# w_out*phi tiles converted around the border of chunks 0 and 1, and g of chunk 1 in the buffer of chunk 0's x

## The chip, the cores and the metric

The kernel runs on one core of a Trainium2 chip. The metric is the device time of one execution in microseconds; the time of the kernel before is the median of three runs.

## The reference

Three stages follow each other on 2304 tokens (4 batches of 576) of 512 features: an attention with 8 heads (four local, four strided), a feed-forward layer, and a soft mixture of 8 experts with 4 slots each.

```python
x = attention(q, k, v)                        # masked, 8 heads, (2304, 512)
h = x @ w_in                                  # (2304, 2048)
g = h * (1.0 / (1.0 + np.exp(-1.702 * h)))
x = g @ w_out                                 # (2304, 512)
logits = x @ phi                              # 32 slots
d = softmax(logits, over tokens); slot_input = d.T @ x
for e in range(8):
    slot_out[e] = relu(slot_input[e] @ w1[e]) @ w2[e]
c = softmax(logits, over slots)
return c @ slot_out
```

## The kernel before

The kernel never forms `g @ w_out` for the tokens. It folds w_out into its neighbours: the logits are g times `wp = w_out @ phi`, and the slot inputs are (weighted sums of g) times w_out. The raw weights arrive as 64-bit words (`wraw`), of which `narrow` (lines 279 to 290) makes fp32 numbers with two ACT instructions (L286, L287) and two DVE instructions (L288, L289). It is called for three kinds of tiles, 16 of each: `wc` (w_in), `wt` (w_out transposed, for `wp`) and `wo` (w_out, written back to DRAM for the late stage by `store_wo`). Only w_in is further split by `split` into two fp32r halves, on ACT (L306) and GpSimd (L307).

The middle of the program is a list of 80 steps (line 325): five chunks of tokens (four of 512, the last of 256) times 16 tiles f of the hidden dimension. Step i does `gemm1(c, f)`: 12 products into one of two PSUM buffers `h`, then tanh on ACT (L356) and a gate on DVE (L357), which leaves g of 128 hidden units. Step 0 is (0, 0), step 16 is (1, 0), step 32 is (2, 0).

g is read twice. `logits` (four f at a time, L372) multiplies it by `wp`, and `g_transpose` (DVE, L380) puts it into the blocks of `gT` for the weighted sums. g of chunk 0 lies in `gT` at f+1 and is transposed to f, so it has to wait for the logits of the tile that lies there. `g_slot` finds a place for g of later chunks: spare places 17, 18 and 16 of `gT`, and three in a tile named `more`, which is opened at step 16.

`wp` is made by `wo_phi(q)` (eight PE instructions L314 on four wt tiles, then an ACT scaling L316) and `wo_phi_sum(q)` (L322 on PE, a copy L323 on ACT), once for each q of 0 to 3. The table `WT` says at which step which wt tile is converted, and `PHI` at which steps wo_phi runs; the logits of chunk 0 follow one step after each. After the last of them `post(0)` starts: maxima, exponentials, the weighted sums `u` (L479) and the accumulators.

Beside the steps runs, a unit per step, the attention of the next batch: batch 1 in chunk 0, batch 2 in chunk 1, batch 3 in chunk 2. Its scores (L176), softmax (L192 to L210), transposes (L225) and values (L244) end with two instructions that split the result into the x tiles of its chunk (ACT L269, DVE L270). Batch 2 covers tokens 1152 to 1727, that is chunk 2 and the first 192 columns of chunk 3. Three pairs of buffers (pool `xp`) take turns: the first loads of q and k, chunk 0, chunk 1, chunk 2, chunk 3, chunk 4, late weights.

`store_wo` converts the 16 wo tiles at even distances from step `ROWS` to step 47.

All loads and stores are issued on SP's queue. Each engine works its queue in order. That order is planned when the program is built: the order of the program is the priority, and an instruction may be put ahead where the plan finds its inputs ready and its engine free. `tc.issue_after` keeps the conversions of wt and wo behind tanh and gate of the step before.

Of the kernel before, what the change touches and what calls it, by code (L numbers as in the profile page):

```python
# [9 lines left out]
F32 = mybir.dt.float32  # L10
# [25 lines left out]
AHEAD = 3  # L36
WT = {2: (0,), 3: (1,), 5: (2,), 6: (3,), 8: (4,), 9: (5,), 10: (6,), 11: (7,), 12: (8,), 13: (9,), 14: (10,), 15: (11,),
      16: (12,), 17: (13, 14), 18: (15,)}
ROWS = 22
PHI = [8, 13, 17, 19]  # L40
COLS = [(0, 256), (256, 128), (384, 128)]
# [7 lines left out]
def tile_kernel(ctx: ExitStack, tc: tile.TileContext, lqk, lv, sqk, sv, wraw, phi, wexp, cst, out):  # L49
# [5 lines left out]
    keep = ctx.enter_context(tc.tile_pool(name="keep", bufs=1))  # L55
    xp = ctx.enter_context(tc.tile_pool(name="xp", bufs=3))
    wip = ctx.enter_context(tc.tile_pool(name="wip", bufs=NF // 2))
# [51 lines left out]
    def load_qk(b, hp):  # L109
        src = lqk[b, hp] if hp < 2 else sqk[b, hp - 2]  # L110
        if b == 0 and hp > 1:
            t = xp.tile([P, 2 * SW + HS * P], F32, tag=f"x{hp - 2}", name=f"qkv_{hp}")
            vals[b, hp] = t[:, 2 * SW:]
            t = t[:, :2 * SW]
        else:
            t = att.tile([P, src.shape[1]], F32, tag="qk", name=f"qk_{b}_{hp}")
        nc.sync.dma_start(t, src)
        qkv[b, hp] = t
# [11 lines left out]

    def x_tile(c):
        if c not in xt and c < 4:
            xt[c] = [xp.tile([P, 4, 512], F32R, tag=f"x{e}", name=f"x{e}_{c}") for e in range(2)]
        elif c not in xt:
            t = xp.tile([P, 2, 4, 256], F32R, tag="x0", name=f"x_{c}")
            xt[c] = [t[:, e] for e in range(2)]
        return xt[c]
# [93 lines left out]
    def att_values(b, hp):  # L231
# [19 lines left out]
        for e in range(2):  # L251
            for c, (c0, cn) in enumerate(CHUNKS):
                if local:
                    s0 = S * b + QT * cut * e
                    n = QT * (cut, NTL - cut)[e]
                    lo, hi = max(s0, c0), min(s0 + n, c0 + cn)
                    if lo >= hi:
                        continue
                    src = av[e][:, lo - s0:hi - s0]
                    dsts = [x_tile(c)[k][:, hp, lo - c0:hi - c0] for k in range(2)]  # L260
                else:
                    a0, a1 = max(0, (c0 - S * b) // STR), min(RA, (c0 + cn - S * b) // STR)
                    if a0 >= a1:
                        continue
                    r0, nr = (0, 3 * HS) if e == 0 else (3 * HS, STR - 3 * HS)
                    lo = S * b + STR * a0 - c0
                    src = av[e][:, :RA * nr].rearrange("p (r a) -> p r a", a=RA)[:, :, a0:a1]
                    dsts = [x_tile(c)[k][:, hp, lo:lo + STR * (a1 - a0)].rearrange("p (a r) -> p r a", r=STR)[:, r0:r0 + nr, :] for k in range(2)]
                nc.scalar.copy(dsts[0], src)  # L269
                nc.vector.tensor_tensor(dsts[1], src, dsts[0].bitcast(F32), op=ALU.subtract)  # L270
# [58 lines left out]
    def g_slot(c, f):  # L329
        if c == 4 and f >= 6:  # L330
            ks = (NF + 1, NF + 2) if 8 <= f < 12 else (NF, NF + 1)
            k = next((k, h) for k in ks for h in range(2) if k not in taken and (k, h) not in taken)
            taken.add(k)
            where[c, f] = k
            return slots[k[0]][:, 256 * k[1]:256 * k[1] + 256]
        k = f + 1 if c == 0 else next(k for k in [*range(NF + 1, NF + 6), NF] if k in slots and k not in taken)
        assert k not in taken
        taken.add(k)
        where[c, f] = k
        return slots[k]  # L340
# [45 lines left out]
    def moe_step(i):  # L386
# [17 lines left out]
        else:  # L404
            for _ in range(1 if c == 0 else 2 if c > 1 or f > 5 else 4):
                if todo and todo[0][1] not in taken and (c > 1 or gdone.get(todo[0])):
                    g_transpose(*todo.pop(0))
        gemm1(c, f)
        todo.append((c, f))
        for q in range(4):  # L410
            if i == PHI[q]:
                wo_phi_sum(q)
            if i == PHI[q] + 1:
                logits(0, 4 * q)
                if q == 3:
                    side.append(post(0))
                    next(side[-1])
        if i > NF and f % 4 == 0:
            pc, pf = steps[i - 4]
# [247 lines left out]
    for i, (c, f) in enumerate(steps):  # L667
# [3 lines left out]
        if (c, f) == (1, 0):  # L671
            wc_es.close()
            morep = gt_es.enter_context(tc.tile_pool(name="morep", bufs=1))
            more = morep.tile([P, 3, 512], F32, tag="more", name="more")
            slots.update({NF + 3 + k: more[:, k] for k in range(3)})
        if (c, f) == (1, 4):
            raw_es.close()
# [12 lines left out]
        if (c, f) == (3, 2):  # L690
# [3 lines left out]
            for _ in range(6):  # L694
                load_ex(e1p, "e")
            for e in (1, 0, 1):
                load_ex(xp, f"x{e}")
        if (c, f) == (4, 1):
            for e in range(2):
                load_ex(xp, f"x{e}")  # L700
        moe_step(i)
# [14 lines left out]
    for s in side:  # L716
        for _ in s:
            pass
    load_ex(xp, "x0")
    c = len(CHUNKS) - 1  # L720
# [43 lines left out]
    load_ex(e1p, "e")  # L764
    load_ex(xp, "x1")
    h1 = {}
# [65 lines left out]
    for e in range(2):  # L832
        load_ex(xp, f"x{e}")
    expand1(0, 1)
    for e in range(2):
        load_ex(xp, f"x{e}")
    load_ex(wip, "wi")
# [99 lines left out]
```

## Time and profile before

| | us |
|---|---|
| median of 3 runs | 414.33 |
| lowest and highest run | 413.97, 415.26 |
| the profiled execution | 415.33 |
| its span, first to last instruction | 413.5 |

The profile comes from that one execution. The span falls into these stages: attention of batch 0 to about 34 us, gemm1 of chunk 0 to 115, of chunk 1 to 192, of chunk 2 to 262, of chunk 3 to 317, of chunk 4 to 350, then the experts and the output. A window gives the busy time of each engine within a stretch; a group gives the instructions of one line with their mean duration in ns; the chain is the work that ended last, followed back from the end, and its shares of a window say on which engine the time of that stage lay.

### The profile page before, as it was taken

What the parts mean: (1) busy time and instruction counts of PE and PEld (TensorE: products, weight loads), DVE (VectorE), ACT (ScalarE), POOL (GpSimd) and SP (SyncE); (2) the same over time, 40 slices, a digit from 0 to 9 for tenths busy, and PEclk for the clock granted to TensorE, in tenths of its full rate; (3) what the DMA queues carried; (4) which work ended last, traced back from release to release, by engine and by line L of the source; (5) the groups of instructions that cost most, each with busy time, mean ns of one, the idle gap of its engine ahead of it and who ended that gap; (6) DMA issues with size and microseconds to landing.
All of it is one profiled execution on the core that took longest, in us unless ns stands there. A gap on an engine that the chain in (4) does not pass through costs nothing.

```text
span 413.5 us, 9788 instructions
## 1 busy us (share of the span) xinstructions
PE 387.9 (94%) x3930; PEld 269.4 (65%) x3935; DVE 267.6 (65%) x569; ACT 224.8 (54%) x668; POOL 52.4 (13%) x64
## 2 busy tenths in 40 slices
PE   8998998897999999989999999999999999799992
PEld 3656766664776657857767685776778788333682
DVE  2679887799688668868677878547454666412132
ACT  2899789998876546675854758321212222310141
POOL 0433333432310100010110101000000000010000
PEclk9999899999999999999999999999999999999997
DMA  8966477766731422546752442596002899879998
GB/s 237 390 216 212 138 229 238 226 214 229 232 128 43 165 78 98 179 164 211 265 201 78 139 170 101 207 366 268 2 0 103 313 379 334 316 292 406 419 391 259
DMA packets 27917, 89.26 MB, mean 216 GB/s; under 512 B 2400, under 2 KB 9696, under 8 KB 23776
## 3 DMA queue, kind: packets, MB, share of 16 engines
q1 hardware_dynamic: 27872, 88.64, 60.7%
q8 instruction: 31, 0.51, 0.5%
q14 instruction: 14, 0.11, 0.1%
HBM read 79.71 MB, written 8.91 MB: 214 GB/s over the span
## 4 chain that ended last, share of the span: by engine, by line
PE 64%; ACT 16%; DVE 11%; issue 3%; DMA 2%; POOL 2%; SPq 0%; ACTq 0%; DVEq 0%; POOLq 0%
PE h L353 34%; ACT ts L207 7%; PE u L479 5%; PE op L803 4%; PE hp L773 3%; PE lg L372 3%; PE ptp L225 2%; ACT neg L287 2%; PE s L176 2%; PE av L244 2%; DMA qk<-lqk 2%; DVE x L270 2%; PE fp L819 2%; ACT gT L356 2%; DVE wc L289 1%
## 5 line engine op out<-in xcount | busy, mean ns | idle before, releaser
L353 PE MATMUL h<-x,wi 128*128 128x512 f32 (+1 forms) x960 | 217.1, 378 | 2.8 <-DVE gT L357 2.6
L353 PEld LDWEIGHTS h<-x,wi 128*128 128x128 f32 x960 | 165.3, 190 | 52.0 <-issue 14.0
L356 ACT ACTIVATE gT<-h 128x512 f32<-128x512 f32 (+1 forms) x54 | 29.4, 545 | 51.6 <-PE h L353 51.6
L357 DVE SCALAR_TENSOR_TENSOR gT<-gT,h 128x512 f32<-128x512 f32 (+1 forms) x54 | 33.3, 617 | 34.7 <-ACT gT L356 34.3
L207 ACT ACTIVATE ts<-ts,nmx 128x64 f32<-128x64 f32 (+1 forms) x120 | 41.4, 348 | 11.3 <-DVE nmx L202 11.3
L210 POOL TENSOR_TENSOR ts<-ts,sm 128x384 f32<-128x384 f32 (+2 forms) x32 | 27.5, 859 | 156.8 <-DVE sm L209 75.1
L356 ACT ACTIVATE more<-h 128x512 f32<-128x512 f32 (+1 forms) x26 | 14.8, 568 | 40.6 <-PE h L353 40.6
L287 ACT ACTIVATE neg<-raw,ebias 128x512 f32<-128x512 int16 x48 | 36.6, 762 | 0.0
L380 DVE STREAM_TRANSPOSE gT<-gT 128x512 f32<-128x512 f32 (+1 forms) x54 | 34.3, 640 | 1.5 <-PE lg L372 0.3
L307 POOL TENSOR_TENSOR wi<-wc,wi 128x512 fp32r<-128x512 f32 x16 | 22.0, 1374 | 26.0 <-ACT wi L306 17.0
L357 DVE SCALAR_TENSOR_TENSOR more<-more,h 128x512 f32<-128x512 f32 (+1 forms) x26 | 16.9, 651 | 12.6 <-ACT more L356 12.0
L269 ACT CAST x<-av 128x320 fp32r<-128x320 f32 (+20 forms) x54 | 18.9, 400 | 10.9 <-DVE x L270 9.1
L225 PE MATMUL ptp<-cs,ts 128*96 128x128 f32 (+1 forms) x120 | 17.3, 279 | 6.7 <-POOL ts L210 3.7
L479 PE MATMUL u<-gT,dT 32*32 32x512 f32 x576 | 21.4, 597 | 2.0 <-DVE z L537 1.6
L207 ACT ACTIVATION_READ_ACCUMULATOR ts<-ts,nmx 128x1 f32 x120 | 22.5, 188 | 0.0
L270 DVE TENSOR_TENSOR x<-av,x 128x320 fp32r<-128x320 f32 (+20 forms) x54 | 19.9, 394 | 2.6 <-ACT x L269 2.6
L372 PE MATMUL lg<-gT,wp 128*32 128x512 f32 (+1 forms) x100 | 19.9, 566 | 1.1 <-DVE gT L357 1.1
L225 PEld LDWEIGHTS ptp<-cs,ts 128*96 128x96 f32 (+1 forms) x120 | 13.0, 133 | 11.7 <-POOL ts L210 10.5
L176 PEld LDWEIGHTS s<-qk 64*64 64x64 f32 x552 | 15.8, 136 | 5.9 <-issue 4.4
L176 PE MATMUL s<-qk 64*64 64x96 f32 (+1 forms) x552 | 18.9, 240 | 0.6 <-DMA qk<-lqk 0.6
L380 DVE STREAM_TRANSPOSE gT<-more 128x512 f32<-128x512 f32 (+1 forms) x26 | 17.3, 671 | 1.6 <-PE u L479 1.0
L244 PEld LDWEIGHTS av<-pt,v 96*64 96x64 f32 (+2 forms) x552 | 13.9, 136 | 5.8 <-issue 3.5
(154 smaller groups left out, 475.6 us busy)
## 6 DMA issues: line engine op xcount, KB each, us to landing
ex<-wexp SPq DMA_DIRECT2D x28, 1024.0 KB, 7.0
raw<-wraw SPq DMA_DIRECT2D x48, 511.8 KB, 4.0
qk<-lqk SPq DMA_DIRECT2D x8, 592.0 KB, 5.8
wo_scr<-wo SPq DMA_DIRECT2D x16, 256.0 KB, 2.3
ex<-wo_scr SPq DMA_DIRECT2D x4, 1024.0 KB, 9.8
gT<-wexp SPq DMA_DIRECT2D x4, 1024.0 KB, 6.0
qk<-sqk SPq DMA_DIRECT2D x6, 604.0 KB, 5.2
v<-lv SPq DMA_DIRECT2D x8, 432.0 KB, 5.1
```

What stands on the lines that cost most here:

```text
L176: nc.tensor.matmul(sp[part][o:o + 64, u], t[hs, qo:qo + 64], t[hs, ko + qo:ko + qo + nk], start=not early, stop=not early or part * half + ...
L207: nc.scalar.activation(ts[:, u], src[:, u], AF.Exp, scale=sc, bias=nmx[:, u:u + 1], accum_out=sm[:, u:u + 1])
L210: nc.gpsimd.tensor_tensor(ts, ts, sm[:, :nt].unsqueeze(2).to_broadcast([P, nt, nk]), op=ALU.mult)
L225: nc.tensor.transpose(ptp[:nk, u - a], src, ident)
L270: nc.vector.tensor_tensor(dsts[1], src, dsts[0].bitcast(F32), op=ALU.subtract)
L287: nc.scalar.activation(n, top, AF.Relu, scale=-(2.0 ** 19), bias=ebias)
L353: nc.tensor.matmul(h[:, :N], w[:, we, 128 * kt:128 * kt + 128], x[xe][:, kt, :N], start=n == 0, stop=n == 11)
L356: st["tanh"] = nc.scalar.activation(g[:, :N], h[:, :N], AF.Tanh, scale=0.851).ins
L357: st["gate"] = nc.vector.scalar_tensor_tensor(g[:, :N], g[:, :N], 1.0, h[:, :N], op0=ALU.add, op1=ALU.mult).ins
L372: nc.tensor.matmul(lgs[c][32 * j:32 * j + 32, :N], wp[:, f0 + j, :], gs[c, f0 + j][:, :N], start=f0 == 0, stop=f0 == NF - 4)
L380: nc.vector.transpose(t_slots(c)[:, f, :N], gs[c, f][:, :N])
L479: nc.tensor.matmul(us[a][32 * j:32 * j + 32, :].rearrange("p (t f) -> p t f", f=32), dT[q, 32 * b:32 * b + 32], gT[q, :, 32 * b:32 * b + 3 ...
```

## The change

- `WT`, `PHI`: the first wt tile is converted at step 6 instead of 2, the last two at step 21 instead of the last one at 18. Seven tiles instead of twelve have a step of chunk 0. wo_phi runs at steps 14, 17, 20, 22 instead of 8, 13, 17, 19, and the logits of chunk 0 at 15, 18, 21, 23.
- The logits of chunk 1 for f of 0 to 3 and 4 to 7 run at steps 24 and 25 instead of 20 and 24; the transposes allowed per step in chunk 1 are four while one of chunk 0 is due, then two.
- `ROWS` is 27 instead of 22; the loads of the first wo tiles and the accumulators move from step 20 to step 23.
- The three buffers of `xp` get names (A, B, C) in place of a rotation. Chunk 3's x goes to C (chunk 1's) and not to B. B, chunk 0's, takes the first eight g of chunk 1 (`xg`). The part of batch 2 that belongs to chunk 3 is written to a tile in `more`, and two DMAs on SP copy it to chunk 3's x at step 32; only then does `more` hold g.
- The late weights `ex` are loaded to the same number of buffers under the new names.

```diff
--- before.py
+++ after.py
@@ -34,10 +34,12 @@
 NF = FF // 128
 TFROM = 5
 AHEAD = 3
-WT = {2: (0,), 3: (1,), 5: (2,), 6: (3,), 8: (4,), 9: (5,), 10: (6,), 11: (7,), 12: (8,), 13: (9,), 14: (10,), 15: (11,),
-      16: (12,), 17: (13, 14), 18: (15,)}
-ROWS = 22
-PHI = [8, 13, 17, 19]
+WT = {6: (0,), 9: (1,), 11: (2,), 13: (3,), 14: (4, 5), 15: (6,), 16: (7,), 17: (8, 9), 18: (10,), 19: (11, 12), 20: (13,),
+      21: (14, 15)}
+ROWS = 27
+PHI = [14, 17, 20, 22]
+REGION = "BCACB"
+XG = NF + 6
 COLS = [(0, 256), (256, 128), (384, 128)]
 PARTS = [(0, 2), (2, 4), (6, 4), (10, 4), (14, 4)]
 LAST = [(0, 4), (4, 4), (8, 4), (12, 4), (16, 2)]
@@ -53,7 +55,7 @@
     ps_m = ctx.enter_context(tc.tile_pool(name="ps_m", bufs=5, space=PSUM))
     scr = ctx.enter_context(tc.tile_pool(name="scr", bufs=1, space=bass.MemoryType.DRAM))
     keep = ctx.enter_context(tc.tile_pool(name="keep", bufs=1))
-    xp = ctx.enter_context(tc.tile_pool(name="xp", bufs=3))
+    xp = ctx.enter_context(tc.tile_pool(name="xp", bufs=1))
     wip = ctx.enter_context(tc.tile_pool(name="wip", bufs=NF // 2))
     moe_es = ctx.enter_context(ExitStack())
     moe_ps = ctx.enter_context(ExitStack())
@@ -109,7 +111,7 @@
     def load_qk(b, hp):
         src = lqk[b, hp] if hp < 2 else sqk[b, hp - 2]
         if b == 0 and hp > 1:
-            t = xp.tile([P, 2 * SW + HS * P], F32, tag=f"x{hp - 2}", name=f"qkv_{hp}")
+            t = xp.tile([P, 2 * SW + HS * P], F32, tag=f"xA{hp - 2}", name=f"qkv_{hp}")
             vals[b, hp] = t[:, 2 * SW:]
             t = t[:, :2 * SW]
         else:
@@ -128,11 +130,13 @@
 
     xt = {}
 
-    def x_tile(c):
+    def x_tile(c, b=None):
+        if (c, b) == (3, 2):
+            return [st["x3"][:, e] for e in range(2)]
         if c not in xt and c < 4:
-            xt[c] = [xp.tile([P, 4, 512], F32R, tag=f"x{e}", name=f"x{e}_{c}") for e in range(2)]
+            xt[c] = [xp.tile([P, 4, 512], F32R, tag=f"x{REGION[c]}{e}", name=f"x{e}_{c}") for e in range(2)]
         elif c not in xt:
-            t = xp.tile([P, 2, 4, 256], F32R, tag="x0", name=f"x_{c}")
+            t = xp.tile([P, 2, 4, 256], F32R, tag=f"x{REGION[c]}0", name=f"x_{c}")
             xt[c] = [t[:, e] for e in range(2)]
         return xt[c]
 
@@ -257,7 +261,7 @@
                     if lo >= hi:
                         continue
                     src = av[e][:, lo - s0:hi - s0]
-                    dsts = [x_tile(c)[k][:, hp, lo - c0:hi - c0] for k in range(2)]
+                    dsts = [x_tile(c, b)[k][:, hp, lo - c0:hi - c0] for k in range(2)]
                 else:
                     a0, a1 = max(0, (c0 - S * b) // STR), min(RA, (c0 + cn - S * b) // STR)
                     if a0 >= a1:
@@ -265,7 +269,7 @@
                     r0, nr = (0, 3 * HS) if e == 0 else (3 * HS, STR - 3 * HS)
                     lo = S * b + STR * a0 - c0
                     src = av[e][:, :RA * nr].rearrange("p (r a) -> p r a", a=RA)[:, :, a0:a1]
-                    dsts = [x_tile(c)[k][:, hp, lo:lo + STR * (a1 - a0)].rearrange("p (a r) -> p r a", r=STR)[:, r0:r0 + nr, :] for k in range(2)]
+                    dsts = [x_tile(c, b)[k][:, hp, lo:lo + STR * (a1 - a0)].rearrange("p (a r) -> p r a", r=STR)[:, r0:r0 + nr, :] for k in range(2)]
                 nc.scalar.copy(dsts[0], src)
                 nc.vector.tensor_tensor(dsts[1], src, dsts[0].bitcast(F32), op=ALU.subtract)
 
@@ -333,7 +337,10 @@
             taken.add(k)
             where[c, f] = k
             return slots[k[0]][:, 256 * k[1]:256 * k[1] + 256]
-        k = f + 1 if c == 0 else next(k for k in [*range(NF + 1, NF + 6), NF] if k in slots and k not in taken)
+        order = [*range(NF + 1, NF + 6), NF]
+        if c == 1:
+            order = [*range(XG, XG + 8), *order] if f < 9 else [*order, *range(XG, XG + 8)]
+        k = f + 1 if c == 0 else next(k for k in order if k in slots and k not in taken)
         assert k not in taken
         taken.add(k)
         where[c, f] = k
@@ -402,7 +409,7 @@
             while todo and todo[0][0] < c and todo[0][1] not in taken:
                 g_transpose(*todo.pop(0))
         else:
-            for _ in range(1 if c == 0 else 2 if c > 1 or f > 5 else 4):
+            for _ in range(1 if c == 0 else 4 if todo and todo[0][0] == 0 else 2):
                 if todo and todo[0][1] not in taken and (c > 1 or gdone.get(todo[0])):
                     g_transpose(*todo.pop(0))
         gemm1(c, f)
@@ -415,7 +422,9 @@
                 if q == 3:
                     side.append(post(0))
                     next(side[-1])
-        if i > NF and f % 4 == 0:
+        if i in (PHI[3] + 2, PHI[3] + 3):
+            logits(1, 4 * (i - PHI[3] - 2))
+        if i >= 28 and f % 4 == 0:
             pc, pf = steps[i - 4]
             logits(pc, pf)
             if f == 0:
@@ -671,9 +680,15 @@
         if (c, f) == (1, 0):
             wc_es.close()
             morep = gt_es.enter_context(tc.tile_pool(name="morep", bufs=1))
+            st["x3"] = morep.tile([P, 2, 4, 192], F32R, tag="more", name="x3t")
+            xg = [xp.tile([P, 4, 512], F32, tag=f"xB{e}", name=f"xg_{e}") for e in range(2)]
+            slots.update({XG + k: xg[k // 4][:, k % 4] for k in range(8)})
+        if (c, f) == (2, 0):
+            for e in range(2):
+                nc.sync.dma_start(x_tile(3)[e][:, :, :192].bitcast(F32), st["x3"][:, e].bitcast(F32))
             more = morep.tile([P, 3, 512], F32, tag="more", name="more")
             slots.update({NF + 3 + k: more[:, k] for k in range(3)})
-        if (c, f) == (1, 4):
+        if i == PHI[3] + 1:
             raw_es.close()
             accp = acc_es.enter_context(tc.tile_pool(name="accp", bufs=1))
             sp_["p"] = accp
@@ -693,11 +708,11 @@
             e1p = ctx.enter_context(tc.tile_pool(name="e1p", bufs=6, side="right"))
             for _ in range(6):
                 load_ex(e1p, "e")
-            for e in (1, 0, 1):
-                load_ex(xp, f"x{e}")
+            for x in ("xB1", "xA0", "xA1"):
+                load_ex(xp, x)
         if (c, f) == (4, 1):
             for e in range(2):
-                load_ex(xp, f"x{e}")
+                load_ex(xp, f"xC{e}")
         moe_step(i)
         if (c, f) == (4, 12):
             cT = morep.tile([P, 3, 512], F32R, tag="more", name="cT")
@@ -716,7 +731,7 @@
     for s in side:
         for _ in s:
             pass
-    load_ex(xp, "x0")
+    load_ex(xp, "xB0")
     c = len(CHUNKS) - 1
     man = ctx.enter_context(ExitStack())
     man.enter_context(tc.manual_schedule(engines={mybir.EngineType.PE, mybir.EngineType.DVE, mybir.EngineType.Activation}))
@@ -762,7 +777,7 @@
     hzt = e1p.tile([P, 2, 8, P], F32, tag="e", name="hz")
     hc = e1p.tile([P, 4, 512], F32, tag="e", name="hc")
     load_ex(e1p, "e")
-    load_ex(xp, "x1")
+    load_ex(xp, "xB1")
     h1 = {}
 
     def expand1(G, n):
@@ -830,10 +845,10 @@
     for k in range(0, 8, 2):
         nc.gpsimd.memset(hzt[:, :, k:k + 2], 0.0)
     for e in range(2):
-        load_ex(xp, f"x{e}")
+        load_ex(xp, f"xA{e}")
     expand1(0, 1)
     for e in range(2):
-        load_ex(xp, f"x{e}")
+        load_ex(xp, f"xC{e}")
     load_ex(wip, "wi")
     load_ex(wip, "wi")
     hidden_t(0, 0)
```

## Rows read from the trace of the kernel before

**Rows 1.** the page: busy time and share of the span of PE

```profile
PE 387.9 (94%) x3930; PEld 269.4 (65%) x3935; DVE 267.6 (65%) x569; ACT 224.8 (54%) x668; POOL 52.4 (13%) x64
```

**Rows 2.** windows by stage: gemm1 of chunks 0, 1, 2; busy us of each engine

```profile
core 0: us, PE busy (x) PEld busy (x) DVE busy (x) ACT busy (x) POOL busy (x), PEclk, DMA share, GB/s
34.00:115.00 81.00, 72.00 (x562) 51.19 (x561) 68.35 (x124) 70.67 (x189) 26.25 (x24) 0.96 0.66 215
115.00:192.00 77.00, 75.55 (x764) 53.00 (x768) 58.32 (x120) 49.18 (x152) 7.05 (x10) 1.00 0.38 127
192.00:262.00 70.00, 68.71 (x714) 49.65 (x707) 54.37 (x113) 46.00 (x145) 7.04 (x10) 1.00 0.46 156
```

**Rows 3.** chain of work by line, 34 to 115 us, then 115 to 192

```profile
by line: ACT ts L207 12.8%; PE h L353 12.1%; ACT neg L287 9.6%; DVE wc L289 6.8%; issue 6.2%; ACT wc L286 5.1%; ACT wt L286 5.1%; DVE x L270 4.7%; DVE wc L288 4.1%; ACT gT L356 4.1%; DVE wt L289 4.1%; ACT wi L306 3.8%; POOL ts L210 3.5%; DV
...
by line: PE h L353 49.1%; PE lg L372 6.6%; PE u L479 6.0%; PE av L244 4.5%; PE wp L314 3.7%; PE s L176 3.6%; PE ptp L225 3.0%; ACT gT L356 3.0%; ACT ts L207 2.7%; DVE gT L357 2.7%; issue 2.6%; PE wq L322 2.1%; DVE x L270 2.0%; DVE wo L289 1
```

**Rows 4.** groups by line, 34 to 115 us: busy, mean ns, idle before; ACT, then DVE

```profile
L287 ACT ACTIVATE neg<-raw,ebias 128x512 f32<-128x512 int16 x25 | 19.0, 761 | 0.0
L286 ACT ACTIVATE wt<-raw,ebias 128x512 f32<-128x512 int16 x12 | 9.3, 772 | 0.0
L316 ACT ACTIVATE wpT<-wp 128x512 f32<-128x512 f32 x2 | 1.2, 589 | 0.0
L323 ACT COPY wp<-wq 128x128 f32<-128x128 f32 x2 | 0.5, 264 | 0.0
...
L289 DVE SCALAR_TENSOR_TENSOR wt<-raw,wt 128x512 uint32<-128x512 uint32 x12 | 11.8, 984 | 0.1
L288 DVE TENSOR_TENSOR wt<-wt,neg 128x512 int32<-128x512 f32 x12 | 9.0, 753 | 1.8 <-ACT neg L287 1.7
L380 DVE STREAM_TRANSPOSE gT<-gT 128x512 f32<-128x512 f32 x6 | 4.2, 704 | 0.0
```

**Rows 5.** groups by line, 115 to 192 us, DVE

```profile
L380 DVE STREAM_TRANSPOSE gT<-gT 128x512 f32<-128x512 f32 x18 | 12.6, 703 | 0.7 <-PE lg L372 0.3
L289 DVE SCALAR_TENSOR_TENSOR wt<-raw,wt 128x512 uint32<-128x512 uint32 x5 | 3.4, 675 | 0.1
L288 DVE TENSOR_TENSOR wt<-wt,neg 128x512 int32<-128x512 f32 x4 | 2.7, 686 | 1.4 <-ACT neg L287 1.4
```

**Rows 6.** chain in order of time, chunk 1: start us, us, what

```profile
115.97 2.96 PE h L353 x12
118.93 1.00 PE wp L314 x8
119.93 5.67 PE h L353 x24
125.60 0.84 PE wq L322 x8
127.45 0.99 PE lg L372 x8
...
129.29 0.61 PE av L244 x14
```

**Rows 7.** PE in order of time, second group of wo_phi; the wait in brackets

```profile
99.53 1.04 PE L314 MATMUL wp<-wt,phs 128*32 128x512 f32 x2 [1.75 <-DVE wt L289]
100.81 4.58 PE L353 MATMUL h<-x,wi 128*128 128x512 f32 x12 [0.24 <-DVE gT L357]
```

**Rows 8.** window behind that wait, columns as in rows 2

```profile
102.50:104.00 1.50, 1.50 (x5) 1.11 (x4) 1.17 (x5) 1.50 (x6) 0.56 (x1) 0.50 0.31 101
```

**Rows 9.** groups by line, 192 to 262 us, ACT

```profile
L286 ACT ACTIVATE wo<-raw,ebias 128x512 f32<-128x512 int16 x10 | 7.6, 762 | 0.0
```

**Rows 10.** DMA issues: count, KB each, median us to landing

```profile
v<-sv SPq DMA_DIRECT2D x6, 384.0 KB, 4.4
```

**Rows 11.** in order of time at step 32: gemm1 on PE, tanh on ACT

```profile
192.72 3.03 PE L353 MATMUL h<-x,wi 128*128 128x512 f32 x12
...
199.01 0.57 ACT L356 ACTIVATE more<-h 128x512 f32<-128x512 f32 x1
```

## The prediction

> **What bounds the kernel now.** I read the page first, then the windows by stage, then the chain of work cut at the same borders, and last the groups of one line in each stage. The page puts PE at 94% of the span [rows 1]. That is an average, and it hides the stage that matters. gemm1 of chunk 0 runs from 34 to 115 us, of chunk 1 to 192, of chunk 2 to 262 [rows 2]. In chunk 0, ACT is busy 70.67 of 81.0 us (87%) and DVE 68.35 (84%). PE's 72.00 includes products stretched by waiting: an undisturbed step takes 2.71 (5.67 for two steps less 2.96 for one [rows 6]), 16 of them 43.4. The chain says the same: in chunk 0 its largest parts are exponentials (ACT L207, 12.8%), the decoding of raw weights (L286 to L289) and only 12.1% gemm1. In chunk 1 it is 49.1% gemm1, and nearly all else that is large in it is PE too [rows 3]. So until 115 us ACT and DVE set the pace; from there PE does, with ACT at 64% and DVE at 76% of that stage.
>
> **The change part by part.**
>
> *Conversions leave chunk 0.* A wt tile is the `narrow` of one piece of w_out: two ACT and two DVE instructions. Before, 12 of the 16 are converted before 115 us [rows 4]; by the new table seven are (steps 6, 9, 11, 13, 14 twice, 15). Five tiles leave. ACT: 772 + 761 = 1.53 us a tile, 7.65 in all; one of two groups of `wo_phi` and `wo_phi_sum` goes too (0.59 + 0.26), so 8.5. DVE: 753 + 984 = 1.74 a tile, 8.7; and the six transposes of chunk 0's g (4.2) can't run before the logits of step 15, so 12.9. What is that worth? Upper bound: ACT keeps its 87% share, (70.67 - 8.5)/0.87 = 71.3, a gain of 9.7. Lower bound: only what stands on the chain goes. wt has 5.1% (L286), 4.1% (L289) and 12/25 of the 9.6% of neg, 4.6%: 13.8% of 81 us is 11.2 for 12 tiles, 4.7 for five. PE doesn't forbid the upper value: chunk 1 does on PE what chunk 0 does and more (weighted sums 6.0% of 77, 4.6 us; three groups of logits more, 3.0), with gaps of some 8 us (the pieces of ACT and DVE in its chain, 3.0, 2.7, 2.7 and 2.0% [rows 3]), so chunk 0's own work on PE is near 61. I take -8.0, nearer the upper bound, because ACT's share is what the windows show for the whole stage, while the chain, one path, leaves out the near-critical DVE work that goes too. Nothing before 45 us is touched, so the span to there stays.
>
> *Two PE groups move into chunk 1.* The second group of wo_phi (step 13 to 17), its sums and one logits group more fall after 115 us: 1.00 + 0.84 + 0.99 = +2.8 us [rows 6]. PE is the bound there, so I count it whole; if it falls into gaps that chunk 1 has, it is 0.
>
> *Chunk 1 takes the five tiles.* There a tile costs DVE 686 + 675 = 1.36 us [rows 5], less than in chunk 0, where POOL is busy 26.25 us and not 7.05 [rows 2]. The stage gets 7.65 + 0.85 us on ACT and 6.8 on DVE; counted by the rules of `g_transpose` it gets 28 transposes for 23, at 703 ns +3.5. It loses two w_out tiles, since store_wo starts at step 27 and not 22 (four for six by step 31): -3.0 on ACT, -2.7 on DVE. So ACT 54.7 and DVE 65.9 in about 81 us: 68% and 81%, below the 84 to 87% at which they set the pace of chunk 0. That cover holds, and I cost it at 0; where it doesn't, the price is the slower rival's.
>
> *Less lead for the last tile of a group.* Before, the last wt of groups 0 to 2 is converted two steps ahead of wo_phi, that of group 3 one; after, all four have one step. PE is in order: a wo_phi that waits holds the next gemm1, hence tanh and gate, and h has two buffers. Near price: group 3 was held between its sixth and seventh product from 129.29 to 129.90, and PE filled that with products of the attention [rows 6]: 0.6 us at most. Far price: group 1, in chunk 0, waited 1.75 us for DVE, and the next gemm1 took 4.58 [rows 7] for the 3.03 of an undisturbed one in that view [rows 11]: 3.3 in all. The extra 1.55 is the clock, which stood at 0.50, the 1.2 GHz level, at 102.5 to 104, after PE had idled [rows 8]. Three groups now stand in chunk 1, and one 0.6 was there before: 3 x 0.6 - 0.6 = +1.2; far end 3 x 3.3 - 0.6 = +9.3. I take the near one, since rows 6 is the same stage with the same lead.
>
> The Trainium skill (TensorE: Matmul & The Clock Gate, section "What's actually happening") says that the array's clock falls to 1.2 GHz after idling and comes back only after sustained work. It speaks against a change that lets PE wait more often; the trace agrees (0.50 after the idle stretch), and by it alone the waits would cost the far end.
>
> *w_out denser.* 16 tiles over steps 27 to 47 instead of 22 to 47; chunk 2 gets 12 for 10 [rows 9]. Two tiles are 3.0 us of ACT. ACT has 46.0 of 70 there, but the softmax comes in bursts. From 0 to +3.0; I take +1.0. What would be late then are exponentials behind wo.
>
> *Storage.* g of chunk 1 goes to the buffer of chunk 0's x, which is free when gemm1 of step 15 has ended, before the first tanh of step 16: 0. Batch 2's 192 columns for chunk 3 wait in `more` and are copied by two DMAs of 384 KB at step 32, as chunk 1's x is only then free. On SP they hold batch 3's next loads (v, qk), first needed four steps later, and the raw w_out loads. The first g of chunk 2 goes to `more`, so its tanh on ACT, and behind it exponentials, wait for the landing. Nearest row: 384 KB of v, 4.4 us [rows 10]; one after the other 8.8. gemm1 of step 31 ends about 1 us before that of step 32 begins at 192.72, and that tanh starts at 199.01 [rows 11], 7 us later, because exponentials are in front: hidden, 0; at 8.8 it costs 1.8. The Trainium skill (DMA: Bandwidth & Descriptors, section "Anatomy of one DMA — SWDGE (gpsimd) path") has a fit of 2.0 us plus bytes over 436 GB/s; an estimate from it for both copies is 3.8 us, hidden as well, and no run here shows such a copy. The other moves (accumulators opened at step 23, the buffers of the late weights renamed) keep their number and lie off the path: 0.
>
> *Sum.* -8.0 + 2.8 + 1.2 + 1.0 = -3.0. The profiled execution took 415.33 us (span 413.5 and 1.8 around it), so 412.3 for such a one. The median of the three runs, 414.33, is 1.0 below it: 411.3.
>
> **The rivals.** *More gain:* chunk 0 gives 9.7, the 2.8 of PE falls into chunk 1's gaps of some 8 us, and w_out costs 0. -9.7 + 1.2 = -8.5: 405.8. For it: ACT and DVE are relieved together. Against: steps 13 to 15 get four tiles, where ACT then has no less to do than before.
>
> *A wash:* chunk 0 gives only the chain's 4.7, because the exponentials and the w_in conversions that stay bound it anyway; -4.7 + 2.8 + 1.2 + 1.0 = +0.3: 414.6. This is also what comes out if the planned order of the queues leaves conversions where they are, so that the change does not do what it says.
>
> *Slower:* PE's wait for the last tile of each group, in chunk 1, at the far price with the low clock behind it: -8.0 + 2.8 + 1.0 + 9.3 = +5.1: 419.4. It decides from w on where 3w - 0.6 exceeds 4.2, that is from 1.6 us a group. For it: DVE at 81% and a lead of one step in all groups. Against: the one group with that lead in that stage lost 0.6.
>
> **How the numbers follow.** The forecast has 0.42, its own range 408.5 to 413.5; more gain 0.20; a wash 0.18; slower 0.20, anywhere from 414 to 420. A difference of 0.3% (1.24 us) is about what a measurement of this kernel tells from none. Faster, below 413.1: 0.39 + 0.20 + 0.03 = 0.62; within: 0.03 + 0.13 = 0.16; slower, above 415.6: 0.22. The range takes in nearly all of "more gain" and the nearer part of "slower", and the far ends of w_out (+2.0 on the sum) and of the copy (+1.8): 405.5 to 416.5.
>
> **What would show it.** In the changed kernel the tanh of step 15, which closed chunk 0 at 115.0, should stand near 107, ACT's share up to there at 85% or more. From there to the last gemm1 of chunk 1 should be about 81 us for 77, with wo_phi on the chain and waits for `wt` under 1 us a group. gemm1 of chunk 2 should take some 71 for 70, and the tanh that waits for the copy should follow exponentials and not a DMA. From 262 us on nothing should differ but the offset. The prediction is wrong if chunk 0 still ends after 110, or if a granted clock of 0.5 appears in chunk 1.

## The result and the profile after

The changed kernel takes 409.74 us (median of four runs, 409.12 to 411.03) beside 414.38 for the kernel before: a ratio of 0.9889 with a 95% interval of 0.986 to 0.9919, a gain of 4.6 us. The forecast was 411.3, a gain of 3.0, and faster by more than 0.3% had the largest chance; 409.74 lies within the forecast's own range of 408.5 to 413.5.

First the windows of the changed kernel by stage, as [rows 2] show them for the kernel before: gemm1 of chunk 0, 1, 2, then to the end of gemm1, then the rest. The borders are the first product and the last end of each chunk's gemm1. A line number is that of the run's own file, so L360 here is L353 of the kernel before.

```profile
core 0: us, PE busy (x) PEld busy (x) DVE busy (x) ACT busy (x) POOL busy (x), PEclk, DMA share, GB/s
33.40:104.30 70.90, 63.79 (x530) 48.56 (x530) 60.53 (x108) 63.83 (x178) 26.19 (x24) 0.98 0.62 201
104.30:185.30 81.00, 79.50 (x788) 53.09 (x784) 64.52 (x131) 53.38 (x159) 7.01 (x10) 1.00 0.46 149
185.30:256.70 71.40, 69.40 (x714) 49.62 (x714) 56.34 (x117) 48.62 (x148) 7.05 (x10) 1.00 0.51 176
256.70:344.80 88.10, 87.86 (x727) 66.87 (x728) 48.47 (x100) 19.84 (x44) 0.00 (x0) 1.00 0.60 225
344.80:409.30 64.50, 54.94 (x750) 29.67 (x750) 18.68 (x59) 14.60 (x34) 1.92 (x4) 0.94 0.90 342
```

The same stages in a second profile of the same kernel:

```profile
34.20:104.50 70.30, 63.67 (x529) 48.49 (x530) 60.39 (x108) 63.71 (x178) 26.15 (x24) 0.98 0.62 204
104.50:185.50 81.00, 79.52 (x788) 53.12 (x791) 64.61 (x132) 53.37 (x159) 7.00 (x10) 1.00 0.45 149
185.50:255.60 70.10, 68.28 (x713) 49.46 (x714) 56.36 (x117) 48.66 (x148) 7.04 (x10) 1.00 0.53 178
```

| stage | before, us | term of the sum | after, first profile | second |
|---|---|---|---|---|
| to the first gemm1 | 34.0 | 0 | 33.4 | 34.2 |
| chunk 0 | 81.0 | -8.0 | 70.9 (-10.1) | 70.3 (-10.7) |
| chunk 1 | 76.8 | +2.8 +1.2 | 81.0 (+4.2) | 81.0 (+4.2) |
| chunk 2 | 69.9 | +1.0 | 71.4 (+1.5) | 70.1 (+0.2) |
| chunks 3 and 4 | 88.1 | 0 | 88.1 | 88.2 |
| the rest | 63.7 | 0 | 64.5 (+0.8) | 64.6 (+0.9) |

(before, with the borders of its own gemm1: 34.0, 115.0, 191.8, 261.7 and 349.8.) The gain is where it was looked for, in chunk 0. In these profiles it is larger than forecast, though the 81.0 of before is the longest of three profiles of this stage (79.4 to 81.0, below). Chunk 1 pays 4.2 for the forecast's 4.0, though not for the reasons given, as the runs below show. ACT's share of chunk 0 went from 87 to 90%, 63.83 of 70.9.

Most of the last row is no part of the change. There the weighted sums of chunk 4 ran at a granted clock of 0.55 (the mean of the window 349.6 to 353.4, so nearly all of it at the 1.2 GHz level) instead of 1.00, and took 3.75 us for the 2.34 of before:

```profile
349.60:353.40 3.80, 3.77 (x68) 1.16 (x72) 2.10 (x11) 0.34 (x2) 0.00 (x0) 0.55 0.50 209
```

```profile
349.63 3.75 PE L488 MATMUL u<-gT,dT 32*32 32x512 f32 x64 [1.57 <-DVE z L546]
```

The same products took 3.50 in the second profile. Of all fourteen profiles of this document, which are the same program in this place, ten have 2.34 and four 3.50 to 3.83. PE waits 1.57 us before the products in all of them, so what decides is open.

### The profile page after: what moved, and what is told of

The parts are those of the page before. It is cut to its first block, busy times and chain, and to the rows that moved or that the text cites. A ratio compares the mean times of both kernels' runs of the same rounds, so it can differ in the third digit from the quotient of the medians.

```text
span 409.3 us, 9816 instructions
## 1 busy us (share of the span) xinstructions
PE 386.1 (94%) x3935; PEld 267.1 (65%) x3935; DVE 268.8 (66%) x569; ACT 225.0 (55%) x668; POOL 52.3 (13%) x64
## 4 chain that ended last, share of the span: by engine, by line
PE 66%; DVE 13%; ACT 13%; issue 3%; DMA 2%; POOL 1%; SPq 0%; ACTq 0%; DVEq 0%; POOLq 0%
PE h L360 32%; ACT ts L211 7%; PE u L488 5%; PE op L818 4%; PE hp L788 3%; PE lg L379 3%; PE s L180 3%; PE ptp L229 3%; DVE wc L293 2%; PE av L248 2%; PE fp L834 2%; DVE x L274 2%; PE busy L89 2%; DMA x<-x3t 1%; ACT neg L291 1%
## 5 line engine op out<-in xcount | busy, mean ns | idle before, releaser
L360 PE MATMUL h<-x,wi 128*128 128x512 f32 (+1 forms) x960 | 216.2, 377 | 2.8 <-DVE gT L364 1.9
L360 PEld LDWEIGHTS h<-x,wi 128*128 128x128 f32 x960 | 164.0, 189 | 50.6 <-issue 16.6
L363 ACT ACTIVATE gT<-h 128x512 f32<-128x512 f32 (+1 forms) x51 | 27.6, 542 | 48.2 <-PE h L360 48.1
L364 DVE SCALAR_TENSOR_TENSOR gT<-gT,h 128x512 f32<-128x512 f32 (+1 forms) x51 | 31.3, 614 | 29.8 <-ACT gT L363 29.4
L387 DVE STREAM_TRANSPOSE gT<-gT 128x512 f32<-128x512 f32 (+1 forms) x51 | 32.2, 635 | 3.0 <-PE lg L379 1.7
L363 ACT ACTIVATE more<-h 128x512 f32<-128x512 f32 (+1 forms) x19 | 10.7, 562 | 35.8 <-PE h L360 35.3
L364 DVE SCALAR_TENSOR_TENSOR more<-more,h 128x512 f32<-128x512 f32 (+1 forms) x19 | 12.1, 637 | 10.4 <-ACT more L363 10.2
L273 ACT CAST x<-av 128x320 fp32r<-128x320 f32 (+18 forms) x48 | 17.0, 413 | 3.4 <-PE av L248 1.9
L274 DVE TENSOR_TENSOR x<-av,x 128x320 fp32r<-128x320 f32 (+18 forms) x48 | 18.2, 405 | 0.5 <-ACT x L273 0.5
L293 DVE SCALAR_TENSOR_TENSOR wc<-raw,wc 128x512 uint32<-128x512 uint32 x16 | 17.9, 1117 | 0.1
L379 PE MATMUL lg<-gT,wp 128*32 128x512 f32 (+1 forms) x94 | 17.5, 563 | 0.0
L212 DVE TENSOR_SCALAR sm<-sm 128x5 f32<-128x5 f32 (+2 forms) x32 | 6.1, 189 | 17.1 <-ACT ts L211 17.0
```

The source lines that it names most:

```text
L360: nc.tensor.matmul(h[:, :N], w[:, we, 128 * kt:128 * kt + 128], x[xe][:, kt, :N], start=n == 0, stop=n == 11)
L363: st["tanh"] = nc.scalar.activation(g[:, :N], h[:, :N], AF.Tanh, scale=0.851).ins
L364: st["gate"] = nc.vector.scalar_tensor_tensor(g[:, :N], g[:, :N], 1.0, h[:, :N], op0=ALU.add, op1=ALU.mult).ins
L379: nc.tensor.matmul(lgs[c][32 * j:32 * j + 32, :N], wp[:, f0 + j, :], gs[c, f0 + j][:, :N], start=f0 == 0, stop=f0 == NF - 4)
L387: nc.vector.transpose(t_slots(c)[:, f, :N], gs[c, f][:, :N])
```

## The experiments

Stage lengths below are read as in the table. One profile has to be read with care: chunk 0 of the kernel before took 81.0 us, and 79.6 and 79.4 in two variants that hardly touch it (the storage alone, and the second wo_phi a step later).

**What are five conversions worth in chunk 0?**

```diff
         for k in WT.get(i, ()):
+            if k in (1, 2, 5, 6, 9):
+                continue
...
-conv.pop((4 * q + kt, 1))
+wts[min(kt, len(wts) - 1)]
```

> The kernel before, with the conversions and loads of five w_out*phi tiles of chunk 0 (1, 2, 5, 6, 9) left out; their products take a tile that is there. It isolates the first term of the sum. Theory (ACT and DVE set the pace of chunk 0, so what leaves them shortens it): gemm1 of chunk 0 ends at 105 to 108 instead of 115.0, nothing after it changes, total 404.5 to 407.5. Rival (only what stood on the chain is worth anything): 4.7 us, the chunk ends near 110, total 409.7.

407.10 beside 415.02, ratio 0.9776 (0.9727 to 0.9824): 7.9 us. Chunk 0 took 72.1:

```profile
34.00:106.10 72.10, 67.10 (x562) 49.60 (x562) 61.21 (x115) 64.26 (x179) 26.66 (x24) 0.98 0.61 205
```

Chunks 1 and 2 kept their 76.5 and 70.0. So the theory holds: the conversions alone, with the transposes and both PE groups left in place, give most of what the change gave in this stage, and the chain's share (4.7) was too low a measure. The loads of these tiles go with their conversions here and were not left out by themselves.

**Which engine sets the pace of chunk 0?** Two sisters, each with about 9 us less on one engine.

```diff
+        if k == 1 and f < 12:
+            n = t
+        else:
             nc.scalar.activation(n, top, AF.Relu, scale=-(2.0 ** 19), bias=ebias)
```

> The kernel before, with one of the two ACT instructions (the one that writes neg) left out for the 12 wt tiles of chunk 0: 12 x 0.76 = 9.1 us of ACT less, all DVE instructions kept. With its sister run it tells which engine sets the pace of chunk 0. Theory (ACT, by its share of 87%): chunk 0 shortens by 6 to 9 us from 79.5 to 81, total 406 to 409. Rival (DVE, or the hand-overs between the two): by 0 to 4.

```diff
+        if k != 1 or f >= 12:
             nc.vector.tensor_tensor(t.bitcast(I32), t, n, op=ALU.subtract)
```

> The kernel before, with one of the two DVE instructions (the subtraction) left out for the 12 wt tiles of chunk 0: 12 x 0.753 = 9.0 us of DVE less, all ACT instructions kept. Theory (ACT sets the pace): chunk 0 shortens by 0 to 4 us, total 410.5 to 414.5. Rival (DVE sets it): by 6 to 9.

Without 9.1 us of ACT: 410.72 beside 414.57, ratio 0.9899 (0.9871 to 0.9927), 3.9 us by the medians, 3.0 to 5.3 by the interval. Without 9.0 us of DVE: 410.18, ratio 0.9909 (0.9878 to 0.9939), 4.4 us by the medians, 2.5 to 5.1 by the interval. The windows of chunk 0, ACT's first:

```profile
33.40:109.50 76.10, 68.77 (x562) 50.81 (x558) 69.64 (x125) 63.80 (x177) 27.51 (x24) 0.96 0.67 228
```

```profile
33.80:112.70 78.90, 71.81 (x560) 52.47 (x558) 58.65 (x113) 69.93 (x189) 24.90 (x24) 0.94 0.68 221
```

The profiled execution of the second took 413.46, 3.3 above the median of its runs, and its chunk 0 shows only 0.5 to 2.1 us of gain, so the totals count. ACT's run is in its rival's range (0 to 4), DVE's at the edge of the same range. The theory of ACT alone falls: by the medians it gave 0.42 us for each us of instructions taken off it, DVE 0.49. With their intervals both are 0.3 to 0.6, so the two are not told apart. Neither sets the pace by itself. With ACT relieved, DVE is busy 69.64 of 76.1 us (92%); with DVE relieved, ACT 69.93 of 78.9 (89%). That they hand work to each other, tile by tile, fits this.

Two things go into these prices. ACT's instructions overlap at their ends, so that 9.1 us of them took only 6.9 off its busy time (70.67 to 63.80). And DVE did not stay as it was when ACT was relieved: its second instruction on the wc tiles went from 872 ns to 1156, which fits what the run without GpSimd's instruction shows below.

```profile
L292 DVE SCALAR_TENSOR_TENSOR wc<-raw,wc 128x512 uint32<-128x512 uint32 x14 | 16.2, 1156 | 0.0
```

**Does the second wo_phi's wait cost anything by itself?**

```diff
-PHI = [8, 13, 17, 19]
+PHI = [8, 14, 17, 19]
```

> The kernel before, with the second wo_phi at step 14 instead of 13, three steps after its last tile's conversion and not two. In the trace of before it waited 1.75 us for DVE, and the clock stood at 0.50 in the gemm1 behind it. Theory (that wait and the low clock are a loss of their own, which the change also removed and which my sum did not credit): 1.5 to 3 us of chunk 0 go, total 411.5 to 413. Rival (PE was ahead there, ACT and DVE set the end of the chunk all the same): 413.8 to 414.8.

415.59 beside 415.02, ratio 1.0013 (0.9985 to 1.0041): nothing. Its trace shows why. PE in order of time, the place of [rows 7]:

```profile
99.63 4.38 PE L353 MATMUL h<-x,wi 128*128 128x512 f32 x12 [3.01 <-DVE gT L357]
...
105.13 1.06 PE L314 MATMUL wp<-wt,phs 128*32 128x512 f32 x8
```

```profile
100.00:101.00 1.00, 1.00 (x3) 0.76 (x3) 1.00 (x3) 1.00 (x8) 0.00 (x0) 0.50 0.53 188
```

The wait for `wt` is gone, and gemm1 waits 3.01 us for a gate of DVE instead. The clock is at 0.50, the 1.2 GHz level, behind that as well, and its 12 products take 4.38. So the wait costs nothing by itself: its name changed, and the total did not. The low clock stayed, so this run does not price it. The chain of before speaks against a price: while those products run (100.81 to 105.39) it lies on DVE and GpSimd, and PE comes onto it only behind them.

```profile
101.40 0.15 DVE wt L288
...
102.00 0.68 DVE wc L289
102.69 0.60 DVE wt L289
...
103.44 1.29 POOL wi L307
104.73 0.69 POOL ts L210
...
105.47 0.87 PE ptp L225 x6
```

**The storage alone.** The changed file with the old tables:

```diff
-WT = {6: (0,), 9: (1,), 11: (2,), 13: (3,), ...
-ROWS = 27
-PHI = [14, 17, 20, 22]
+WT = {2: (0,), 3: (1,), 5: (2,), 6: (3,), ...
+ROWS = 22
+PHI = [8, 13, 17, 19]
...
-        if i in (PHI[3] + 2, PHI[3] + 3):
-            logits(1, 4 * (i - PHI[3] - 2))
+        if i in (20, 24):
+            logits(1, i - 20)
```

> The changed storage alone: buffers A, B, C, g of chunk 1 in chunk 0's x, the copy of batch 2's columns at step 32, with the tables WT, PHI and ROWS of before. Theory (the storage only makes room; the copy's wait on tanh of step 32 costs about 0.5): total 414.5 to 415.5, chunk 0 ends at 115 as before. Rival (the larger room for g itself helps chunk 1, by up to 2): 412 to 413.5.

415.05 beside 415.02, ratio 0.9985 (0.9956 to 1.0013): no difference by the medians, neither a gain from the room nor a loss; the interval leaves room for 1.8 us of gain. The changed kernel has the same storage and is faster, so the gain is that of the tables.

**What do the conversions cost in chunk 1?**

```diff
         for k in WT.get(i, ()):
+            if i >= NF and k not in (8, 12):
+                continue
```

> The changed kernel, with the conversions and loads of seven of the nine wt tiles that it converts from step 16 on left out (only 8 and 12 of them stay); their products take a tile that is there. It isolates what the moved tiles cost in chunk 1. Theory (PE sets the pace there and the conversions are covered): chunk 1 shortens by 0 to 2 of its 81 us, total 408 to 410. Rival (they cost there what they gave in chunk 0): chunk 1 shortens by 5 to 10, total 400 to 405.

408.20 beside 415.02, ratio 0.9819 (0.9779 to 0.9859). Chunk 1 took 78.0 for 81.0:

```profile
107.20:185.20 78.00, 77.19 (x789) 53.09 (x792) 55.90 (x118) 44.49 (x145) 7.05 (x10) 1.00 0.31 106
```

3.0 us for seven tiles, 0.43 each; a tile is 1.53 us of ACT and 1.36 of DVE. Chunk 0 was longer in this profile than in the changed kernel's (72.1 for 70.3 and 70.9), so the totals differ by less, 1.5 to 2.1 by the medians and 0.7% by the ratios. The price lies between the theory (0 to 2) and the rival (5 to 10), and the theory's "covered" is wrong.

**What does PE work cost in chunk 1?**

```diff
-        for kt in range(4):
-            nc.tensor.matmul(pw[32 * kt:32 * kt + 32], phs[:, kt, :], conv.pop((4 * q + kt, 1)), ...
+        for _ in range(3 if q else 1):
+            for kt in range(4):
+                nc.tensor.matmul(pw[32 * kt:32 * kt + 32], phs[:, kt, :], conv[4 * q + kt, 1], ...
```

> The changed kernel with the four products of the second, third and fourth wo_phi, all in chunk 1, done three times over, so 24 PE instructions a group for 8: at 1.00 us for 8, 6.0 us of PE work more in that chunk and nothing else. It tells what PE work costs there. Theory of the prediction (PE is the bound, count it whole): chunk 1 at 87 for 81 us, total near 416. Rival (chunk 1 has gaps in which PE work falls; with seven tiles left out and both PE groups kept the chunk took 78.0 for the 76.8 of before): 83 to 85, total 411.5 to 414.

413.55 beside 414.82, ratio 0.9957 (0.9933 to 0.9982), 3.2 above the changed kernel as run beside it (410.32, next). Chunk 1 took 84.4 for 81.0:

```profile
104.60:189.00 84.40, 83.41 (x837) 54.68 (x836) 64.80 (x132) 53.94 (x159) 7.28 (x10) 1.00 0.42 142
```

The added work is less than the 6.0 us expected. A group of 24 products takes 2.78 us where one of 8 takes 1.06, here first in this run and then in the changed kernel:

```profile
109.49 2.78 PE L319 MATMUL wp<-wt,phs 128*32 128x512 f32 x24
```

```profile
109.09 1.06 PE L318 MATMUL wp<-wt,phs 128*32 128x512 f32 x8
```

That is 1.72 more a group, about 5.2 for three, of which 3.4 were paid, two thirds. PE was busy for 79.50 of 81.0 us without it, and its idle time fell only from 1.5 to 1.0, so most of the rest went into time that had counted as busy. The chunk is within the rival's range, and counting PE work whole is too much.

**The changed kernel again**, for a second profile:

> The changed kernel itself once more, beside the three runs of this call, and as a second profile: chunk 0 took 81.0 us in the profile of before and 79.6 and 79.4 in two kernels whose chunk 0 does nearly the same, so one profile is good to some 1.5 us in that stage. Theory (chunk 0 gives about 8.5, and part of the 10.2 between the first two profiles is chance): chunk 0 at 71 to 72.5, chunk 1 at 80 to 82, chunk 2 at 71 to 72; total 409 to 411. Rival (10.2 is the size): chunk 0 at 70 to 71.

410.32 beside 414.82, ratio 0.9886 (0.9851 to 0.9922). Chunk 0 took 70.3 and, in five variants with the same tables for it, 70.6 to 72.1 (four of them 70.6 or 70.7). The theory (71 to 72.5) is missed: the stage is steady after the change, and of the 10 us some 1.6 may be chance, on the side of before.

**The copy's wait.**

```diff
+        if (c, f) == (2, 0):
+            order = [XG + 7]
```

> The changed kernel with the first g of chunk 2 in a place of chunk 0's x and not in the tile from which the copies read, so no tanh waits for the copies. It tells what that wait costs. Theory (the trace has tanh of step 32 released by the landing at 192.96, and steps 32 to 35 take 19.5 for 19.0 us): these steps fall to 19.0, total 0.3 to 0.7 below the changed kernel. Rival (exponentials were about to end there anyway, as before): no difference in these steps.

410.38, ratio 0.9881 (0.9845 to 0.9916), as the changed kernel run beside it (410.32). Steps 32 to 35 took 19.2 us, against 19.5 in the changed kernel and 19.0 before. The wait is real, 0.3 to 0.5 us at that place, and too small to be seen in the total.

**The denser w_out.**

```diff
-ROWS = 27
+ROWS = 24
```

> The changed kernel with the w_out tiles spread from step 24 on and not 27. It tells what the denser w_out costs. Theory (it costs chunk 2 about 1.0, all in its last third, 28.1 to 29.1 us, and chunk 1 has room): that third falls to 28.1 to 28.6, chunk 1 grows by less than 0.5, total 0.5 to 1 below the changed kernel. Rival (chunk 1 is as full): chunk 1 grows by 1 or more, total the same or higher.

408.34 beside 414.82, ratio 0.9826 (0.9797 to 0.9855), 2.0 below the changed kernel run beside it by the medians (their intervals just touch). The windows of chunks 1 and 2:

```profile
104.00:185.00 81.00, 79.57 (x789) 53.07 (x792) 65.87 (x135) 54.62 (x161) 7.00 (x10) 1.00 0.51 168
185.00:254.50 69.50, 68.51 (x713) 49.59 (x714) 54.95 (x113) 47.28 (x146) 7.04 (x10) 1.00 0.48 158
```

Chunk 1 is no longer for it (81.0), chunk 2 is 69.5 for 71.4 and 70.1. So the profiles put 0.6 to 1.9 of the 2.0 us into chunk 2; the stage behind gemm1, where the clock differs as told above, is shorter by another 1.4. In the first profile of the changed kernel ACT waited in chunk 2 for raw w_out itself:

```profile
ACT wo L290 <- DMA raw<-wraw: 2.9, 2, 2.0
```

That line is in neither kernel with `ROWS = 24`, and not in the second profile of the changed one. The four other variants with `ROWS = 27` have it, with 0.7, 0.9, 2.5 and 2.6 us. Where it is 2.5 or more, chunk 2 took 71.4 to 71.7; with 0, 0.7 and 0.9 it took 70.1, 69.9 and 71.4. Loads that come just in time at the denser pace, and late in some executions, fit this; the load's queue was not changed by itself.

**Both together**, `ROWS = 24` and the first g of chunk 2 in chunk 0's x:

> The changed kernel with both: w_out tiles from step 24 on, and the first g of chunk 2 off the tile that is copied. Theory (the gain of the first, 2 us and 0.6% in its run, holds; the second gives up to 0.3): 407.5 to 409 beside a kernel before at 414.8, a ratio of 0.981 to 0.985. Rival (the 0.6% was chance): 0.986 to 0.990, as the changed kernel.

408.25 beside 414.57, ratio 0.986 (0.984 to 0.988). By its median it is, with `ROWS = 24` alone (408.34), the fastest here that leaves nothing out: 6.3 us under the kernel before, and some 1.5 to 2 under the changed one. The total is in the theory's range, but the ratio is at the near end of the rival's, and its interval reaches into that of the changed kernel (0.986 to 0.9919): that `ROWS = 24` gains is likely, not shown. Steps 32 to 35 took 19.1 us with and without the other place for g, so that part gave nothing.

**GpSimd and DVE.** In chunk 0 one DVE instruction became longer by the change: the second one on the wc tiles. In the kernel before and in the changed one:

```profile
L289 DVE SCALAR_TENSOR_TENSOR wc<-raw,wc 128x512 uint32<-128x512 uint32 x14 | 12.2, 872 | 0.1
```

```profile
L293 DVE SCALAR_TENSOR_TENSOR wc<-raw,wc 128x512 uint32<-128x512 uint32 x14 | 16.5, 1178 | 0.1
```

```diff
-        nc.gpsimd.tensor_tensor(w[:, 1], t, w[:, 0].bitcast(F32), op=ALU.subtract)
...
-w[:, we, 128 * kt:128 * kt + 128]
+w[:, 0, 128 * kt:128 * kt + 128]
```

> The changed kernel, with GpSimd's subtraction for the low half of w_in left out (the products take the high half in its place). DVE's second instruction on the wc tiles took 0.872 us each in chunk 0 of before and 1.178 in the changed kernel, 0.69 where GpSimd is quiet. Theory (they are held up by GpSimd's instruction on the same tiles): it falls to 0.69 to 0.75 each, that is some 6 us of DVE, and chunk 0 shortens by 1 to 4 of its 70.6 us. Rival (the lengthening has another cause): it stays above 1.0.

406.94 beside 414.57, ratio 0.9819 (0.9797 to 0.9842). Without GpSimd's instruction:

```profile
L293 DVE SCALAR_TENSOR_TENSOR wc<-raw,wc 128x512 uint32<-128x512 uint32 x14 | 9.6, 684 | 0.1
```

```profile
34.40:100.40 66.00, 61.84 (x528) 47.42 (x530) 52.81 (x107) 62.83 (x177) 7.04 (x10) 1.00 0.67 216
```

0.684 each, 6.9 us of DVE, and chunk 0 took 66.0 for 70.6, more than the 1 to 4 expected. The lengthening is GpSimd's doing; the 4.6 us are not its price alone, since the 19 us of GpSimd's own work and the wait for its result are gone as well. The Trainium skill (SBUF — State Buffer, section "Who interferes with whom") says that a DVE instruction with two inputs in SBUF contends with a GpSimd instruction that reads SBUF, because its second input comes through a read interface that the two share. The trace agrees in kind: 1.178 us with GpSimd's instruction and 0.684 without.

## Why the prediction came out right, and where its steps were off

**What bounds the kernel.** Right as to the stages: taking work off ACT and DVE shortens chunk 0, and from the first gemm1 of chunk 1 on PE is the closest to a bound. But going by ACT's share was too simple for chunk 0 (each of two engines is worth about half), and "PE is the bound there, so I count it whole" for chunk 1 (PE work is worth 3.4/5.2 = 0.65).

**-8.0 in chunk 0 was somewhat small: 8.5 to 10.7 came**, from 79.4 to 81.0 before to 70.3 and 70.9 after. The step that was off is the choice between the bounds by ACT's share alone. The upper bound took the durations of ACT's instructions, 8.5, off its busy time; as they overlap, the busy time fell by 6.8 (70.67 to 63.83). At the share of 87% that the bound holds fixed, this gives 73.2 us, a gain of 7.8. The rest came as the share rose to 90%, which fits that DVE was relieved too. That the bound of 9.7 lies among the measured gains is luck. The lower bound leaves out the subtraction on the wt tiles (L288), 2.2% of that chain; with it five tiles are 5.4 and not 4.7, still below the 7.9 that they gave.

With the worth measured above, 0.42 for ACT and 0.49 for DVE, the step's own amounts give 0.42 x 7.65 + 0.49 x 8.7 = 7.5 for five tiles (7.9 was measured); with the moved group's copies, 0.42 x 0.85 = 0.4, and the transposes, 0.49 x 3.5 = 1.7, together 9.6. Five transposes left chunk 0 and not six: the first of the stage, at 42.6 us before and 42.0 after, has no logits to wait for. The intervals of the two worths are wide, so this sum fits without proving its parts. More directly, chunk 0 took 72.1 with the five conversions gone and 70.3 to 70.9 with the whole change, so what left beside them is worth 1.2 to 1.8. The prediction counted the DVE work and gave it no weight. That the transposes are the larger part of this is worked out so; they were not moved by themselves. DVE's busy time fell from 68.35 to 60.53, by 7.8 for a planned 12.9: 0.7 is the sixth transpose, and the wc instructions grew by 14 x 0.306 = 4.3. What the change takes from DVE, GpSimd partly took back.

**The wait and low clock of the second wo_phi**, [rows 7] and [rows 8], vanished with the change, which could have been a gain that the sum had failed to credit. The run with that wo_phi a step later says no for the wait: it was slack of PE in a stage of ACT and DVE. For the low clock only the chain says so.

**+2.8 for two PE groups and +1.2 for waits were too much, and 0 for the conversions in chunk 1 too little.** The three nearly cancelled, which is luck. At 0.65 the groups cost 1.8, if their sums and logits are worth what the products of wo_phi are. No product of wo_phi waits for `wt` in chunk 1: in the list of waits from 104 to 186 us, that pair does not occur, and the chain has the products of the fourth group spread from 132.51 to 139.19 among others, so lead of one step was enough. The five tiles more cost 5 x 0.43 = 2.2: "that cover holds, and I cost it at 0" is the step that failed. DVE at 80% of a stage (64.52 of 81.0) doesn't set its end, yet a conversion that stands in front of a gate or a softmax can delay it. 1.8 + 2.2 = 4.0, for 4.2 measured. The stage also has five transposes more (30 for 25) and two w_out tiles less; the transposes were not tried by themselves.

The chain at the start of chunk 1 shows one such place, in order of time:

```profile
104.88 0.67 ACT wt L290
105.55 0.69 ACT neg L291
...
106.87 1.18 DVE ts L196 x3
108.05 0.60 DVE wt L293
108.65 0.57 DVE nmx L206
...
109.25 1.85 ACT ts L211 x10
...
111.32 1.26 ACT ts L211 x7
112.58 0.49 ACT xg L363
...
113.09 0.70 DVE xg L364
...
113.83 2.56 PE h L360 x10
```

A wt tile's four instructions stand between the scores and the exponentials, the tanh stands behind these, and gemm1 waits for its gate. For nine us the chain isn't on PE, though PE is busy with other work for most of it.

**+1.0 for w_out in chunk 2** was about right: 1.5 and 0.2 in two profiles; undoing three of its five steps, to `ROWS = 24`, gave 2.0 in the total of one run. That late raw loads, not exponentials, would be behind it was not foreseen.

**The copy: 0 was right in the total, for a wrong reason.** The exponentials of [rows 11] were to hide it. They ended earlier, and the landing released the tanh:

```profile
185.17 0.71 SPq L688 DMA_DIRECT2D x<-x3t  x1
```

```profile
186.22 0.34 SPq L304
...
186.64 0.58 SPq L280
...
187.32 5.48 DMA x<-x3t
...
192.96 0.04 ACT more L363
```

The first copy was issued at 185.17. The second stood behind a store and a load of w_out on SP, 2.15 us later, and took 5.48 to land, for the 4.4 of [rows 10]. ACT was idle for 0.4 us. With `ROWS = 24` nothing stood between the two: the second was issued 0.77 us after the first and landed at 190.45, and the tanh behind it waited for exponentials alone.

```profile
185.12 1.39 SPq L688 DMA_DIRECT2D x<-x3t  x2
```

```profile
192.17 0.58 ACT L363 ACTIVATE more<-h 128x512 f32<-128x512 f32 x1
```

So the wait came from what the queue held between the copies, and it goes without another place for g. The fit of the Trainium skill (DMA: Bandwidth & Descriptors, section "Anatomy of one DMA — SWDGE (gpsimd) path") is for DMAs of GpSimd's path, and these were issued on SP. The prediction's estimate from it, 3.8 us for both, does not agree: from first issue to last landing it was 7.6 us (185.17 to 192.80), 2.15 of them the queue.

**The rivals.** "More gain" had the size of chunk 0 right and chunk 1 wrong, since the moved work was not free there. The wash (4.7 from the chain) is refuted by the five tiles, 7.9. "Slower", the wait of wo_phi with the low clock behind it, did not occur: the granted clock is 1.00 through chunk 1.

## What to carry to other kernels

Where two engines hand work to each other, price a us on either by taking it off, or, before that is possible, count both at about half, as it was here, and count all that leaves; the share of the busier one alone leaves out the other. Don't take the durations of instructions off a busy time in which they overlap. In a stage whose bound engine was busy 98%, PE work was paid at two thirds of its length, and the cover for work in front of the softmax or gate was not free: price both, rather than one whole and one at nothing. A wait that vanishes is a gain only if what stands behind it was late: look at what PE waits for next.

## What the runs showed of the hardware that was not expected

The weighted sums of chunk 4, the same 64 products behind the same wait of 1.57 us, took 2.34 us in ten profiles and 3.50 to 3.83 in four, at a granted clock of 0.55 in the changed kernel's: 1.2 to 1.5 us, up to a third of this change's gain, that two profiles can differ by with nothing changed there. A DVE instruction of 0.68 us took 1.18 on average in the changed kernel, where GpSimd worked on the same tiles. It had taken 0.87 in the kernel before, and grew to 1.16 with ACT relieved and to 1.18 by the change.
